# Side transfers on GpSimd's queue, idle products in the outset, and accumulating stores at the end of a one-core S4 and FFN kernel

## The chip, the core and the metric

The kernel runs on one NeuronCore of a Trainium2 chip. Its engines work from their own instruction streams: TensorE (PE in the profile, with the weight loads as PEld), VectorE (DVE), ScalarE (ACT), GpSimd (POOL) and SyncE (SP, which here only issues transfers). A transfer between HBM and the on-chip memory is issued by SP, ACT or POOL, in the order of that engine's stream, and carried out by 16 DMA engines that all queues share. The metric is the device time of one execution in microseconds (us). A second view of the same program, one profiled execution, gives the trace from which all rows here come.

## The reference: what is computed

The input is u of 2048 rows (positions) and D = 576 channels, all float32. With xn the layernorm of u along its channels, the output is the sum of three terms:

```python
x = A_u
xn = _layernorm(x, axis=-1)
return x + _A_ref(xn, A_A_re, A_A_im, A_B_re, A_B_im, A_C_re, A_C_im, A_log_dt, A_Dskip) + _B_ref(xn, B_w1, B_w2)
```

`_A_ref` is a long convolution per channel: a kernel K[d, l], the real part of a sum over 128 complex exponentials, is convolved causally with xn through a Fourier transform of length 4096, and xn times Dskip is added. `_B_ref` is a feed-forward layer, silu(xn w1) w2, with 4608 hidden units.

## The kernel before, in words

**The main stream** is the feed-forward layer, the generator `ffn()`. The hidden units are 36 tiles of 128, taken in 9 chunks of four; the rows are two halves of 1024, each of two blocks of 512. For each chunk and block, `up` makes `ph` = w1 times the transposed xn (L289 to L291), ScalarE takes silu and rounds it (`gf` L297, `gh` L298), VectorE keeps the rest (`gl` L299), and `down` multiplies with w2 into `po` (L318) and adds it to the accumulator `acc` (L323), which began as x itself. float32 operands are split into a high and a low part, with three products for one: that is what `w1h`, `w1l`, `gh`, `gl` are. From the third chunk of the second half on, `wino_ffn` takes the layer with fewer, larger products (lines 427 to 577; weight splits L361 and L362, products L444 and L450, sums `f` such as L519 and L535).

**The side stream** is the generator `side()`, drawn by `weave` at set shares of the main stream's 276 steps. It makes, in this order: layernorm and transposes of x (`phase0`, with `norm`, `normed`, `put_xt`); the convolution kernel (`natural`, `kgen`), whose results go from a `stage` tile to the HBM table `d1k` (L883), while `spread` takes the normalised rows `xr` (L145), transforms them (`u`, L155 to L157) and stores them in `d1u` (L158); 32 spectral steps, which load `ur` and `kr`, multiply, and store `d` (L942); and the tail, which loads `ys` (L993) and makes the last transform, `conv` (L1005).

**Where the halves end.** After the last chunk of the first half `down` stores each accumulator to an HBM table `dr0` (L326), and every second time loads the next pair of x tiles into the freed buffer (L328 through L166). In the tail `load_r0` (L951) brings `dr0` back, `add_conv` adds the convolution to it on VectorE (L1016), and `store` writes the output (L173), 16 tiles of rows in quarters of 32 partitions. The second half's output tiles get their convolution within PSUM: `down` begins `po` with it in the last pass (L305 to L310).

**What sets the order.** The program text gives the order, and the Tile framework's planner (`schedule_with_timeline_sim=True`) moves instructions of each engine within it by its own estimates; `behind(ins)` keeps an instruction after another one, and a pool's number of buffers says how early a load may start. Within an engine, and within a queue, the order is then fixed: an instruction that waits holds up all behind it. SP's queue carries the weights (`w1r` L244 to L246, `w2r` L266), the x tiles, the stores `dxt` (L226) and `dxn` (L227), `xr`, the bases `eb` (L776), `d1k`, `dr0`, `ur`, `kr`, `ys` and part of the output; POOL's queue carries the constants, the very first `w1r`, `d1u`, `d`, the `w` of the second half (L471), the spectral matrices (L892) and output. Dskip is added into one row of `d1k` by an accumulating transfer of POOL (L886).

**The outset.** `side` loads two pairs of x tiles, takes the statistics (L182), scales them (`xn`, on VectorE for even tiles, L191, on ScalarE for odd ones, L196), and PE transposes them (`pt`, L123 and L127), from which ScalarE and VectorE take `xh`, `xl` and the last 64 channels (L124 to L129). Meanwhile `ffn` loads and splits the first weights (`split_w1`, L257 and L259).

```python
    sd = side()
    next(sd)
    fg = ffn()
    next(fg)
    next(sd)
    weave(fg, 276, sd)
```

## Time and profile before

| | |
|---|---|
| time, median of three runs | 1136.37 us (1135.81 to 1136.94) |
| the profiled execution | 1141.59 us, span 1139.8 us |
| granted TensorE clock, mean | 0.990 |
| busy: PE, DVE, ACT, POOL | 1104.0, 955.5, 721.1, 113.4 us |
| moved by the DMA engines | 176.04 MB, mean 154 GB/s |

The span is the time from the first to the last thing that the trace shows; the execution took 1.8 us more. Busy time counts an engine's instructions, not its waits and not the issuing of transfers by SP and ACT; on POOL the issuing shows as busy time, since the engine writes the descriptors itself. A row of the page names line, engine, operation, destination <- sources, and a count; "idle before" is what its engine waited for. The clock column is what the chip's throttle granted to TensorE, as a share of full speed.

### The profile page before, as it was taken

Reading aid. Unit: us, or ns where it says so; the run is one execution under the profiler, and the core shown is the slowest. Engines: PE = TensorE matmul, PEld = TensorE weight load, DVE = VectorE, ACT = ScalarE, POOL = GpSimd, SP = SyncE. Lnnn points to the kernel's source line nnn. Section 1 sums busy time; section 2 is a strip of 40 time slices with the busy share of each in tenths; the row PEclk is TensorE's granted clock in tenths of the full one; section 3 lists DMA queues with packets and bytes.
Section 4 is the critical chain, followed back from the end, with each engine's and each line's share of the span. In section 5 each row is a group of like instructions: output and inputs, shape, how many; then the busy total and the mean of one; then the engine's idle time right before and its main releaser. Section 6 shows DMA issues by size and latency. Waiting matters only on the chain.

```text
span 1139.8 us, 23099 instructions
## 1 busy us (share of the span) xinstructions
PE 1104.0 (97%) x9101; PEld 991.5 (87%) x9101; DVE 955.5 (84%) x1631; ACT 721.1 (63%) x1269; POOL 113.4 (10%) x206
## 2 busy tenths in 40 slices
PE   6999999999999999999989999999999999999798
PEld 5998989888988899899988889999989899998576
DVE  6698898999999999999979988988888888884432
ACT  4665456676677666676747646887867777772210
POOL 1001000000000000000000002112112112210111
PEclk9999999999999999999989999999999999999899
DMA  9456523536263625376844137556455556547964
GB/s 274 131 160 197 165 97 101 144 109 167 83 166 108 188 86 150 109 218 215 230 124 115 54 64 219 153 172 181 141 161 148 171 171 187 176 121 180 260 172 109
DMA packets 171405, 176.04 MB, mean 154 GB/s; under 512 B 88432, under 2 KB 136576, under 8 KB 170656
## 3 DMA queue, kind: packets, MB, share of 16 engines
q1 hardware_dynamic: 150128, 120.91, 38.4%
q0 software_dynamic: 20784, 52.76, 14.7%
q8 instruction: 72, 1.18, 0.4%
q10 hardware_dynamic: 384, 0.89, 0.3%
q14 instruction: 37, 0.30, 0.1%
HBM read 112.00 MB, written 62.60 MB: 153 GB/s over the span
## 4 chain that ended last, share of the span: by engine, by line
PE 52%; DVE 21%; DMA 10%; issue 7%; ACT 7%; SPq 1%; POOL 1%; DVEq 0%; ACTq 0%; POOLq 0%
PE po L318 23%; PE ph L289 12%; DMA w1r<-in_B_w_dram 5%; PE pb L444 3%; DVE acc L323 2%; PE kp L855 2%; PE pc L444 2%; DMA w2r<-in_B_w_dram 1%; DVE th L798 1%; DMA ys<-d 1%; DVE S L834 1%; DVE C L834 1%; PE pb L986 1%; PE pu L986 1%; DVE gl L299 1%
## 5 line engine op out<-in xcount | busy, mean ns | idle before, releaser
L318 PE MATMUL po<-w,gh 128*128 128x288 f32 x2304 | 479.5, 297 | 8.2 <-ACT gh L298 3.8
L318 PEld LDWEIGHTS po<-w,gh 128*128 128x128 f32 x2304 | 378.2, 189 | 26.7 <-issue 5.6
L318 PE MATMUL po<-w,gl 128*128 128x288 f32 x1152 | 337.3, 297 | 0.4 <-DVE gl L299 0.4
L318 PEld LDWEIGHTS po<-w,gl 128*128 128x128 f32 x1152 | 216.2, 189 | 3.9 <-issue 1.4
L323 DVE TENSOR_TENSOR acc<-po,acc 128x288 f32<-128x288 f32 x296 | 130.5, 451 | 61.9 <-PE po L318 60.6
L289 PE MATMUL ph<-xh,w1h 128*128 128x512 f32 (+1 forms) x368 | 99.7, 389 | 0.9 <-ACT xh L124 0.6
L289 PE MATMUL ph<-xl,w1h 128*128 128x512 f32 (+1 forms) x368 | 99.3, 387 | 0.0
L289 PE MATMUL ph<-xh,w1l 128*128 128x512 f32 (+1 forms) x368 | 98.1, 383 | 0.0
L297 ACT ACTIVATE gf<-ph 128x512 f32<-128x512 f32 (+1 forms) x92 | 53.1, 577 | 48.8 <-PE ph L291 36.0
L289 PEld LDWEIGHTS ph<-xl,w1h 128*128 128x128 f32 x368 | 67.7, 192 | 12.9
L289 PEld LDWEIGHTS ph<-xh,w1l 128*128 128x128 f32 x368 | 66.8, 190 | 12.0
L289 PEld LDWEIGHTS ph<-xh,w1h 128*128 128x128 f32 x368 | 65.5, 192 | 11.3 <-ACT xh L124 0.9
L814 ACT ACTIVATE c<-th,magic 128x1040 f32<-128x1040 f32 x36 | 42.0, 1168 | 39.8 <-DVE C L835 31.6
L158 POOL DMA_DIRECT2D d1u<-u x32 | 17.3, 542 | 460.2 <-ACT u L157 460.2
L299 DVE TENSOR_TENSOR gl<-gf,gh 128x512 fp32r<-128x512 f32 (+1 forms) x92 | 60.6, 660 | 2.9 <-ACT gh L298 2.7
L298 ACT CAST gh<-gf 128x512 fp32r<-128x512 f32 (+1 forms) x92 | 55.2, 601 | 10.2 <-PE po L318 9.0
L816 ACT ACTIVATE c<-th 128x1040 f32<-128x1040 f32 x36 | 38.7, 1074 | 31.1 <-DVE th L815 31.1
L361 ACT CAST w1h<-w1r 128x512 fp32r<-128x512 f32 (+2 forms) x56 | 34.5, 619 | 37.1 <-DMA w1r<-in_B_w_dram 36.0
L892 POOL DMA_DIRECT2D m<-in_cm_dram x64 | 34.5, 539 | 223.7 <-PE pu L986 140.3
L362 DVE TENSOR_TENSOR w1l<-w1r,w1h 128x512 fp32r<-128x512 f32 (+2 forms) x56 | 38.3, 685 | 21.7 <-ACT w1h L361 21.7
L834 DVE TENSOR_TENSOR S<-th,C 128x1024 f32<-128x1024 f32 x36 | 43.9, 1219 | 9.8 <-ACT th L817 9.7
L461 DVE TENSOR_TENSOR gl<-gf,gh 128x512 fp32r<-128x512 f32 x56 | 37.8, 687 | 10.8 <-ACT gh L460 10.5
(268 smaller groups left out, 2372.2 us busy)
## 6 DMA issues: line engine op xcount, KB each, us to landing
w1r<-in_B_w_dram SPq DMA_DIRECT2D x35, 512.0 KB, 4.2
dw<-w SPq DMA_DIRECT2D x28, 576.0 KB, 4.7
w<-dw POOLq DMA_DIRECT2D x28, 576.0 KB, 5.8
w2r<-in_B_w_dram SPq DMA_DIRECT2D x44, 288.0 KB, 5.0
d1u<-u POOLq DMA_DIRECT2D x32, 288.0 KB, 2.7
d1k<-stage SPq DMA_DIRECT2D x18, 512.0 KB, 7.0
ur<-d1u SPq DMA_DIRECT2D x32, 288.0 KB, 4.0
kr<-d1k SPq DMA_DIRECT2D x32, 288.0 KB, 3.0
```

Source lines behind the costliest of these rows:

```text
L289: nc.tensor.matmul(ph, w[:, kt, :], v[:, kt, a:e], start=n + kt == 0, stop=False)
L297: nc.scalar.activation(gf, ph, AF.Silu)
L298: pins["gh"] = nc.scalar.copy(gh, gf).ins
L299: pins["gl"] = nc.vector.tensor_sub(gl, gf, gh).ins
L318: pins["pe"] = nc.tensor.matmul(po[:, :HD], gs[g][:, js], ws[:, w, hs], start=n == 0 and j not in begun, stop=n == 3 * len(terms) - 1, ski ...
L323: nc.vector.tensor_add(acc[j][:, hs], po[:, :HD], acc[j][:, hs])
L362: nc.vector.tensor_sub(l[:, :k], src, h[:, :k])
L444: pins["pe"] = nc.tensor.matmul(dst, a[:, kt], v[:, kt], start=start and n == 0, stop=stop and n == 5, skip_group_check=True).ins
L461: pins["gl"] = nc.vector.tensor_sub(gl, gf, gh).ins
L814: nc.scalar.activation(c65, th, AF.Identity, bias=magic)
L816: nc.scalar.activation(c65, th, AF.Abs)
L834: nc.vector.tensor_mul(ov3, t[:, :, 0:64].rearrange("n d (x y) -> n d x y", y=32), mv3)
```

## The change

- Off SP's queue and onto POOL's go the loads of `xr` (16) and `eb` (18), the stores of `dxt` (8), `dxn` (9) and `d1k` (18), and the loads of x at the end of the first half (16). The very first `w1r` goes the other way.
- `dr0` and its loads go. At the end of the first half the accumulators are stored into the output itself, by POOL. The tail's convolutions are made in pairs of tiles, copied from PSUM to a tile `yt` (two buffers) by ScalarE, and stored by POOL with an accumulating transfer, which adds to what the output holds.
- The last pass begins its `po` in other PSUM pools, for two pairs differently.
- Outset: the first pair of x is loaded tile by tile, both of its tiles are scaled on VectorE, and the other x tiles are loaded later; 14 products of a zero matrix run on PE ahead of the first transposes and 5 more after each of the first two tiles; `ffn` and `side` take turns in finer steps, w2 is loaded ahead of the split of w1, and some splits are kept behind other tiles' casts.

```diff
--- before.py
+++ after.py
@@ -81,7 +81,6 @@
     dxn = dram.tile([P, NJ, D], F32, name="dxn")
-    dr0 = dram.tile([8 * P, D], F32, name="dr0")
...
@@ -116,15 +115,16 @@
 
-    def put_xt(xh, xl, x4, src):
+    def put_xt(xh, xl, x4, src, low=None):
...
         nc.scalar.copy(xh, pt)
-        nc.vector.tensor_sub(xl, pt, xh)
+        with behind(low):
+            nc.vector.tensor_sub(xl, pt, xh)
         pt = pss.tile([P, 512], F32, tag="pss", name="pt4")
-        nc.tensor.transpose(pt[:64, :P], src[:, NKT * P:D], ident)
+        pins["pt"] = nc.tensor.transpose(pt[:64, :P], src[:, NKT * P:D], ident).ins
...
@@ -142,7 +142,7 @@
             src = up.tile([P, D], F32, tag="xr", name="xr")
-            nc.sync.dma_start(src, dxn[:, j])
+            nc.gpsimd.dma_start(src, dxn[:, j])
...
@@ -162,15 +162,19 @@
         t = pool.tile([P, 2, D], F32, tag=tag, name=f"{tag}{j}")
-        for ps, v, eng in quarters(xv, engines):
-            eng.dma_start(t[ps], v[:, j:j + 2])
+        for i in range(j, j + 2, 1 if j == 0 else 2):
+            for ps, v, eng in quarters(xv, engines):
+                if j == 0:
+                    eng.dma_start(t[ps, i], v[:, i])
+                else:
+                    eng.dma_start(t[ps], v[:, j:j + 2])
...
 
-    def store(t, j, engines):
+    def store(t, j, engines, **more):
...
         for ps, v, eng in quarters(ov, engines):
-            eng.dma_start(v[:, j:j + 2] if len(t.shape) > 2 else v[:, j], t[ps])
+            eng.dma_start(v[:, j:j + 2] if len(t.shape) > 2 else v[:, j], t[ps], **more)
...
@@ -187,7 +191,7 @@
         for i, j in enumerate(js):
-            if j % 2 == 0:
+            if j % 2 == 0 or n == 1:
...
@@ -200,18 +204,28 @@
         if j0 < 8:
-            xs = load_x(j0, accp, "acc", (nc.sync, nc.scalar) if j0 < 4 else (nc.sync,))
+            xs = load_x(j0, accp, "acc", (nc.sync, nc.scalar) if j0 == 0 else (nc.sync,))
             acc.update(zip(js, xs))
+            yield
...
         if j0:
-            normed(p0, js, xs)
+            with behind(pins["xt1"] if j0 == 2 else None):
+                normed(p0, js, xs)
         else:
-            for j, xj in zip(js, xs):
-                normed(p0, (j,), (xj,))
+            xn = [norm(p0, (j,), (xj,)) for j, xj in zip(js, xs)]
+            last = pins["xn"]
+            for j in js:
+                turned(p0, (j,), xn[j], None if j else last)
+                pins[f"xt{j}s"] = pins["xt_s"]
+                with behind(pins["pt"]):
+                    for _ in range(5):
+                        nc.tensor.matmul(idle[:, :P], zero, zero, start=True, stop=True)
...
     def normed(p0, js, xs):
-        xn = norm(p0, js, xs)
+        turned(p0, js, norm(p0, js, xs))
+
+    def turned(p0, js, xn, low=None):
...
@@ -219,12 +233,12 @@
                 xh, xl, x4 = xts[b]
-                put_xt(xh[:, :, c], xl[:, :, c], x4[:, c], xn[:, i, :])
+                put_xt(xh[:, :, c], xl[:, :, c], x4[:, c], xn[:, i, :], low)
...
                 put_xt(xt[:, 0:4, :], xt[:, 4:8, :], xt[:, 8, :], xn[:, i, :])
-                nc.sync.dma_start(dxt[b - 2][:, :, jj * P:(jj + 1) * P], xt.bitcast(F32))
-        nc.sync.dma_start(dxn[:, js[0]:js[0] + len(js)], xn[:, :len(js)])
+                nc.gpsimd.dma_start(dxt[b - 2][:, :, jj * P:(jj + 1) * P], xt.bitcast(F32))
+        nc.gpsimd.dma_start(dxn[:, js[0]:js[0] + len(js)], xn[:, :len(js)])
...
@@ -240,7 +254,7 @@
             fs = slice(f * P, (f + 2) * P)
-            eng = nc.gpsimd if first and t == 0 else nc.sync
+            eng = nc.sync
...
@@ -253,7 +267,7 @@
                 src = r1[:, :, i * P:(i + 1) * P]
-                with behind(pins.get("gh", pins["xt1s"] if t else None)):
+                with behind(pins.get("gh", pins["xt1s" if t + i else "xt0s"])):
...
@@ -303,8 +317,9 @@
             if half == 1 and c == NCH - 1 and jj % 2 == 0:
-                for i, (pool, tag) in enumerate(((ps2, "ps2"), (ps1, "ps1"))):
-                    begun[j + i] = [pool.tile([P, 512], F32, tag=tag, name="po") for _ in range(2)]
+                pools = (((ps2, "ps2"), (pss, "pss")), ((pss, "pss"),) * 2) if jj == 0 else (((ps2, "ps2"),) * 2, ((ps1, "ps1"),) * 2)
+                for i in range(2):
+                    begun[j + i] = [pool.tile([P, 512], F32, tag=tag, name="po") for pool, tag in pools[i]]
...
@@ -322,10 +337,9 @@
             if half == 0 and c == NCH - 1:
-                rows = slice(j * P, (j + 1) * P)
-                nc.sync.dma_start(dr0[rows, :], acc[j])
                 if j % 2:
-                    acc[7 + j], acc[8 + j] = load_x(7 + j, accp, "acc", (nc.sync,))
+                    store(pairs[j - 1], j - 1, (nc.gpsimd,))
+                    acc[7 + j], acc[8 + j] = load_x(7 + j, accp, "acc", (nc.gpsimd,))
...
@@ -336,10 +350,12 @@
             load_w1(0, 0, t)
+        yield 0
+        for t in range(FT):
+            load_w2(0, 0, t)
...
             split_w1(0, 0, t)
-        for t in range(FT):
-            load_w2(0, 0, t)
+        yield 0
...
@@ -624,7 +640,7 @@
 
-    kl = yp = pa = kfp = tail_at = None
+    kl = yp = pa = kfp = tail_at = zero = idle = None
...
@@ -773,7 +789,7 @@
                     bases.append(kg.tile([P, 2, W, 4], F32, tag="eb", name="eb", bufs=2))
-                    nc.sync.dma_start(bases[-1].rearrange("n g c k -> n g (c k)"),
+                    nc.gpsimd.dma_start(bases[-1].rearrange("n g c k -> n g (c k)"),
...
@@ -880,7 +896,7 @@
                     for gp_ in range(2):
-                        nc.sync.dma_start(kv[gp_, :, :, d0:d0 + NRUN * CH], stage[gp_ * 64:(gp_ + 1) * 64])
+                        nc.gpsimd.dma_start(kv[gp_, :, :, d0:d0 + NRUN * CH], stage[gp_ * 64:(gp_ + 1) * 64])
...
@@ -946,24 +962,19 @@
 
-        r0s = {}
-
-        def load_r0(j):
-            r0s[j] = yp.tile([P, 2, D], F32, tag="r0", name="r0", bufs=2)
-            nc.sync.dma_start(r0s[j], dr0[j * P:(j + 2) * P, :].rearrange("(i p) d -> p i d", p=P))
-
         def last(j):
-            add_conv(j, r0s[j - j % 2][:, j % 2, :])
-            conv_load(j + AHEAD)
-            if j % 2:
-                store(r0s[j - 1], j - 1, (nc.gpsimd,))
-
-        steps, at = [], tail_at[0]
-        for j in range(8):
-            for f in (conv_load, load_r0)[j >= AHEAD:2 - j % 2]:
-                steps.append((at, f, j))
-                at += tail_at[1]
-        steps += [(tail_at[2] + j * tail_at[3], last, j) for j in range(8)]
+            y = yp.tile([P, 2, D], F32, tag="yt", name="yt", bufs=2)
+            py = [[pool.tile([P, 512], F32, tag=tag, name="py") for pool, tag in pools]
+                  for pools in (((ps2, "ps2"), (pss, "pss")), ((pss, "pss"),) * 2)]
+            conv((j, j + 1), py)
+            for i in range(2):
+                for h in range(2):
+                    nc.scalar.copy(y[:, i, h * HD:(h + 1) * HD], py[i][h][:, :HD])
+                conv_load(j + i + AHEAD)
+            store(y, j, (nc.gpsimd,), accum_op=ALU.add)
+
+        steps = [(tail_at[0] + j * tail_at[1], conv_load, j) for j in range(AHEAD)]
+        steps += [(tail_at[2] + j * tail_at[3], last, j) for j in range(0, 8, 2)]
...
@@ -1007,26 +1018,25 @@
 
-    def add_conv(j, dst):
-
-        py = [pss.tile([P, 512], F32, tag="pss", name="py") for _ in range(2)]
-        conv((j,), (py,))
-        for h in range(2):
-            hs = slice(h * HD, (h + 1) * HD)
-            nc.vector.tensor_add(dst[:, hs], py[h][:, :HD], dst[:, hs])
-
...
     def side():
-        nonlocal s4, kl, yp, pa, kfp, tail_at
+        nonlocal s4, kl, yp, pa, kfp, tail_at, zero, idle
         marks = (0.1357, 0.613, 0.855)
-        tail_at = (0.893, 0.003, 0.930, 0.005)
+        tail_at = (0.893, 0.003, 0.932, 0.005)
         with tc.tile_pool(name="pa", bufs=4) as pa:
+            zero = pa.tile([P, P], F32, name="zero", bufs=1)
+            nc.vector.memset(zero, 0.0)
+            idle = ps2.tile([P, 512], F32, tag="ps2", name="idle")
+            for _ in range(14):
+                nc.tensor.matmul(idle[:, :P], zero, zero, start=True, stop=True)
...
                 with behind(pins["xt3"] if js[0] > 2 else None):
-                    phase0(pa, js)
+                    for _ in phase0(pa, js):
+                        if js[0] <= 2:
+                            yield 0
...
@@ -1044,7 +1054,8 @@
                         with behind(pins["gl"]):
-                            phase0(pb, (j, j + 1))
+                            for _ in phase0(pb, (j, j + 1)):
+                                pass
...
@@ -1070,11 +1081,9 @@
 
-    sd = side()
-    next(sd)
-    fg = ffn()
-    next(fg)
-    next(sd)
+    sd, fg = side(), ffn()
+    for g in (sd, fg, sd, fg, sd, fg, sd):
+        next(g)
...
```

## The prediction

> **What bounds the kernel now.** I read the busy shares of the page first, then a table of busy time by stretch, and then, only in the stretches where TensorE (PE) is not full, the chain of work, the waits and the time line of the issuing queue.
>
> ```profile
> PE 1104.0 (97%) x9101; PEld 991.5 (87%) x9101; DVE 955.5 (84%) x1631; ACT 721.1 (63%) x1269; POOL 113.4 (10%) x206
> ```
> ```profile
> 0.00:20.00 20.00, 9.75 (x47) 8.77 (x47) 11.05 (x32) 8.75 (x16) 4.67 (x11) 1.00 0.95 264
> 80.00:100.00 20.00, 18.09 (x102) 15.37 (x101) 16.25 (x35) 9.51 (x17) 1.00 (x1) 0.94 0.65 189
> 560.00:580.00 20.00, 17.00 (x226) 14.96 (x224) 14.94 (x21) 10.92 (x16) 0.55 (x1) 0.97 0.72 221
> 580.00:600.00 20.00, 19.72 (x110) 18.58 (x111) 17.23 (x27) 10.54 (x18) 1.08 (x2) 0.86 0.21 59
> 820.00:840.00 20.00, 17.98 (x103) 16.13 (x102) 14.27 (x29) 13.20 (x29) 3.14 (x6) 0.91 0.38 112
> 1040.00:1060.00 20.00, 18.85 (x150) 15.16 (x148) 6.08 (x13) 2.41 (x5) 1.96 (x4) 1.00 1.11 247
> 1060.00:1080.00 20.00, 12.47 (x81) 9.14 (x82) 9.31 (x21) 5.56 (x11) 3.06 (x6) 0.83 1.04 257
> 100.00:560.00 460.00, 458.59 (x4480) 413.32 (x4479) 437.47 (x660) 305.41 (x458) 19.88 (x35) 1.00 0.50 148
> ```
>
> The columns of the table are busy time (and instructions) of PE, its weight loads, DVE, ACT and POOL, then granted clock, DMA share and GB/s. PE is the bound: in the 460 us between 100 and 560 it idles 1.4 us. What a change of queues can win lies in four places. A stretch loses its idle time and, where the clock is below 1.00, about that part of its busy time: 0 to 20 loses 10.3 us; 80 to 100 1.9 idle + 0.06 x 18.1 = 3.0; 560 to 600 3.3 + 0.5 + 2.8 = 6.6; 1040 to 1080 1.2 + 7.5 + 2.1 = 10.8. A fifth, 820 to 840 (2.0 + 1.6 = 3.6), is touched by no edit. The profiled execution took 1141.59 us with a span of 1139.8, which is 5.2 above the median of the runs; I sum differences against the span and take them off the median.
>
> **The outset.** The time line of the first 20 us:
>
> ```profile
> 1.97 0.81 POOL L244 DMA_DIRECT2D w1r<-in_B_w_dram  x1
> 5.75 1.54 DVE L182 BATCH_NORM_STATS2 st<-acc 128x6 f32<-128x288 f32 x4 [4.82 <-DMA acc<-in_A_u_dram]
> 8.91 1.12 PE L123 MATMUL pt<-ident,xn 128*128 128x128 f32 x4 [8.91 <-DVE xn L191]
> 11.03 1.35 ACT L257 CAST w1h<-w1r 128x640 fp32r<-128x640 f32 x2 [0.22 <-DMA w1r<-in_B_w_dram]
> 12.92 2.07 PE L289 MATMUL ph<-xh,w1h 128*128 128x256 f32 x8 [0.57 <-ACT xh L124]
> 19.08 0.38 ACT L297 ACTIVATE gf<-ph 128x256 f32<-128x256 f32 x1 [2.46 <-PE ph L291]
> 19.31 0.72 PE L289 MATMUL ph<-xh,w1l 128*128 128x256 f32 x4
> ```
>
> Eight such products take 2.07 us at 12.92, and four take 0.72 at 19.31 (eight would be 1.44): until about 19 PE runs at about half speed. The page's clock says 1.00 there, so I go by durations. Two things are late: x (first statistics at 5.75) and the first weights (11.03). Before, two pairs of x (1.18 MB) are asked for ahead of, or beside, the first w1r; after, one pair (0.59 MB), split by tile, so at the 264 GB/s of the stretch 0.59 / 0.264 = 2.2 us less stands ahead. I take the weights and the first products 2.5 us earlier. The idle products cost 14 x 1.12 / 4 = 3.9 us at the slow rate, inside PE's 8.9 us of idleness, and keep PE busy up to the transposes; the 10 others cost 10 x 0.28 = 2.8 slow, some 1.5 fast, in gaps where PE waits for the casts. The work from 12.92 to 18.8 is nearly 6 us at the slow rate; at the fast one, by 1.44 / 2.07, it would be 4.0, less whatever waits then show (the low halves of the weights are split on DVE behind the tiles, and are late next). So 2.5 + 2.0 + 0.5 for a first tile that no longer waits for its partner = 5 us, between 2 (only the data) and 8 (both, with no waits). The memset of the zeros, the extra DMA issues (8 of 72 KB instead of 4 of 144 KB for the first pair) and w2r ahead of the split cost issue time on SP alone.
>
> A row and a rule: the durations change rate near 19 us, 6 us after the products began at 12.92 and with gaps before. The Trainium skill, TensorE: Matmul & The Clock Gate (Part 1), says that the array runs at half rate until it has been busy for about 3.4 us. By it 14 products of 3.9 us just open the gate, and the sum stays; what the rows leave open is whether a gap behind them shuts it again.
>
> **The layernorm of the later tiles (80 to 100).** Chain, then waits:
>
> ```profile
> 79.09 8.09 DMA dxt<-xt
> 91.78 4.15 DMA w2r<-in_B_w_dram
> ```
> ```profile
> ACT xt L124 <- DMA dxt<-xt: 7.4, 2, 6.1
> PE po L318 <- ACT w L275: 1.7, 1, 1.7
> ```
>
> One xt buffer is stored by SP before the next may be written, and w2r stands behind dxt on the queue. After, dxt and dxn go by POOL, so w2r waits for xj loads alone. ACT's wait for the landing stays (one buffer still). I take 2 of the 3.0 us, between +4 (other small waits on dxt too) and a loss of 3 if POOL's store lands later.
>
> **The end of the first half (560 to 600).** Queue of SP, chain, waits:
>
> ```profile
> 563.44 1.00 SPq L326 DMA_DIRECT2D dr<-acc  x1
> 568.85 3.07 SPq L166 DMA_DIRECT2D acc<-in_A_u_dram  x4
> ```
> ```profile
> 573.41 4.97 DMA w2r<-in_B_w_dram
> ```
> ```profile
> ACT w L275 <- DMA w2r<-in_B_w_dram: 6.9, 1, 6.9
> PE po L318 <- ACT gh L298: 3.3, 1, 3.3
> ```
>
> SP stores an accumulator, must wait until that has landed before it loads the next x into the same buffer, and the w2 rows of the next chunk stand behind: SP issues a store at 563.44, the load only at 568.85, w2r at 573.41. ACT waits 6.9 us for it, its gate ops (L298) stand behind in order, PE idles 3.3 and is throttled after. After the change SP has only weights here and runs ahead. The same chain (16 stores of 144 KB, 16 loads) is on POOL, with xr, eb, d1k and d1u behind it: the next late thing would be d1u, for which ACT's next u copy waits (one u1 buffer). I take 4.5 of the 6.6: the rest stays with d1u. Ends: 6 and 0.
>
> **The tail (1040 to 1080).** Chain, waits, SP's queue, the DMA engines in 1030 to 1080, and the landing of today's output stores:
>
> ```profile
> 1040.16 14.89 DMA ys<-d
> 1055.07 10.61 DMA w1r<-in_B_w_dram
> ```
> ```profile
> ACT w1h L361 <- DMA w1r<-in_B_w_dram: 20.9, 1, 20.9
> PE pb L450 <- DVE f L519: 8.1, 1, 8.1
> ```
> ```profile
> 1035.35 0.60 SPq L953 DMA_DIRECT2D r<-dr  x1
> 1039.49 0.62 SPq L953 DMA_DIRECT2D r<-dr  x1
> 1040.16 10.35 SPq L993 DMA_DIRECT2D ys<-d  x6
> ```
> ```profile
> DMA packets 7737, 11.59 MB, mean 232 GB/s; under 512 B 546, under 2 KB 6254, under 8 KB 7734
> ```
> ```profile
> out_dram<-r POOLq DMA_DIRECT2D x16, 144.0 KB, 6.0
> ```
>
> Two r loads stand with the ys ahead of the last w1r; the DMA engines move 232 GB/s at a share of 1.04 to 1.11, so this is bytes. Without the two r (1.18 MB) w1r lands 1.18 / 0.232 = 5.1 us earlier. PE gets there sooner too: the first conv pair comes with tail_at 0.932, and one conv and twelve output products that ran ahead of the wait now stand behind it (order of PE's instructions); that takes back about 2. Half the throttled time (2.1) goes with the shorter wait. 5.1 - 2 + 1.4 = 4.5. Ends: 8 (the bytes of the other r loads help as well) and 0 (the first accumulating store, 0.59 MB that is read and written, stands in the same saturated stretch: 2 x 0.59 / 0.232 = 5.1 us). Copies on ACT (16) take the place of sums on DVE (16 x 0.45); both engines are under half busy there. The 8 stores of dr go (2.4 MB written, with its 2.4 MB read); the stores into the output stay as many, half of them earlier, and 16 come new as accumulating ones. The third copy waits for the first store's landing, since yt has two buffers; the distance between pairs (four steps of 0.005 x about 1130 us are some 11 us) covers a landing of 6.0. If it does not, ACT's gates stand behind it.
>
> **What moves to POOL.** The landing of d1u, then rows of the lines concerned with the issue time in ns (min/median/max):
>
> ```profile
> d1u<-u POOLq DMA_DIRECT2D x32, 288.0 KB, 2.7
> ```
>
> ```profile
> L158 POOL DMA_DIRECT2D d1u<-u x32: 539/539/552, 184.5 to 647.4; - x32
> L886 POOL DMA_DIRECT2D d1k<-in_A_Dskip_dram x1: 858/858/858, 671.8 to 671.8; - x1
> L883 SPq DMA_DIRECT2D d1k<-stage x18: 617/1770/4145, 218.7 to 664.0; - x18
> L244 POOL DMA_DIRECT2D w1r<-in_B_w_dram x1: 808/808/808, 2.0 to 2.0; - x1
> L246 POOL DMA_DIRECT2D w1r<-in_B_w_dram x1: 560/560/560, 3.3 to 3.3; - x1
> ```
>
> L244 on POOL has 512 runs, L246 64: 0.25 us for 448 runs, 0.56 ns a run. d1k<-stage has 4096 runs of 128 B: 0.53 + 4096 x 0.56 ns = 2.8 us each, 18 x 2.8 = 50 us; dxt (1152 runs) 1.2 us, 8 x 1.2 = 9; 16 xr, 18 eb, 9 dxn and 16 acc loads by about 0.55 give 32; the 32 stores to the output replace 16, 16 x 0.5 = 8, and 16 x 0.37 more where they accumulate. All is some 100 us on an engine that is busy 113 of 1140. On PE's path this is worth nothing while d1u leaves in time: the 32 copies of u come from 184.5 to 647.4, one in 14.9 us (in places closer, down to 8), d1u lands in 2.7, and two d1k ahead of it are 5.6, together 8.3, so 0 to 1 us late each of 9 times. Both ends: SP itself takes up to 4.1 us for one, so POOL can be the quicker one, -2; and 9 x 4 = 36 us if descriptors of POOL took 1 ns a run or more. I take 1 us of loss. xr and eb are loaded into one of two buffers ahead of their use, which covers a delay of a step; without it they wait as d1u does.
>
> SP loses 80 of 340 instructions, all between weights; in the full stretches that is worth nothing, since PE idles 1.4 us in 460. The new order of all later instructions, planned anew, has no price in the trace: between +2 (that 1.4 and the like of it) and -6 (one new stall of the size at 560); I take -2. The new PSUM tags of the last pass and the convs in pairs change the order behind 1100 us: 0, between -2 and +1 (a 64-row conv switched in half as often).
>
> **Sum.** 5 + 2 + 4.5 + 4.5 - 1 - 2 = 13 us; I take 12, a part of each first gain being given back by the next wait. Span 1139.8 - 12 = 1127.8; median 1136.4 - 12 = 1124.4.
>
> **Rivals.** (1) Slower: POOL's queue is late. If one d1k takes over 5 us of POOL's time (1.1 ns a run, twice my slope), two of them hold d1u past the next u copy; ACT waits, the gates behind it wait, and PE idles. 9 x 3 = 27 us lost against 13 + 1 gained: 1136.4 + 13 = about 1149. It decides from some 1.6 us a pair on. For it: one u1 buffer and ACT in order; against it: POOL is busy 10% now. (2) The lock: POOL's issues are held up by work of DVE. L158 took 539 to 552 ns in 32 cases beside a DVE that is busy 95% of its time there (437 of 460), so no sign; held by one DVE instruction (437.47 / 660 = 0.66 us) the two d1k and the d1u of each round would leave 2 us later, 9 x 2 = 18, half of it beside other work: 9 of the 12 gone, about 1133. The Trainium skill, SBUF — State Buffer, in the box on "DVE blocks DMA" (section SBUF: two separate sides), says that DMAs from GpSimd cannot get their descriptors written while VectorE runs an op that takes both ports, and advises the other queues: it speaks against the change, and this trace does not bear it out. (3) The tail does not gain: the accumulating stores put back the bytes. 12 - 4.5 = 7.5 gained: about 1129. (4) The outset stays bound by DVE and ACT behind the data: 12 - 4 = 8, about 1128. (5) All gains come near their upper ends, 8 + 4 + 6 + 8 - 1 = 25: about 1112.
>
> **How the numbers follow.** A difference under 0.2% (2.3 us) is no change by the spread of the runs (1135.81 to 1136.94). Forecast, 1118 to 1127: 0.40. (3) and (4), to 1132: 0.25, of which 0.03 no change. (5): 0.10. (2): 0.04, (1) or a new stall of its size elsewhere in the planned order: 0.21, of which 0.04 end within 0.2% and 0.17 beyond. So faster 0.76, same 0.07, slower 0.17. The range leaves out half of (5) and the far half of (1): 1110 to 1141; the forecast's own is 1118 to 1127.
>
> **What would show it.** Outset right: first products near 10 us, the first SiLU near 14 to 15. Weights right: no wait of ACT on w2r near 570, and PE full from 560 to 600. Tail right: the last w1r lands some 5 us earlier and DVE f L535 follows. Wrong: ACT waits for u on d1u with POOL issues of d1k over 5 us; a new idle stretch of PE between 100 and 560; ACT copies of yt that wait for a store.

## The result and the profile after

The changed kernel takes 1141.74 us (median of 11 runs, 1136.29 to 1147.48) beside 1136.34 (1132.36 to 1139.02, 11 runs) of the kernel before. The ratio is 1.0051, with a 95% interval of 1.0031 to 1.0072: slower by about 5 us, where I had forecast 1124.4 in a range of 1110 to 1141. A second comparison (e10 below) gave 1.0037 (1.0020 to 1.0054). The two first profiled executions hide this: 1141.59 us before, 1140.47 after, because the one of before was slower than all its plain runs. A second trace of the kernel before (e0) has a span of 1136.4 us, and I compare with that one too.

Busy shares and DMA packets of the changed kernel:

```profile
PE 1103.6 (97%) x9149; PEld 995.2 (87%) x9149; DVE 950.7 (83%) x1616; ACT 723.7 (64%) x1284; POOL 195.2 (17%) x304
...
DMA packets 85645, 173.68 MB, mean 153 GB/s; under 512 B 10224, under 2 KB 49792, under 8 KB 84896
```

The kernel before had 171405 packets, 88432 of them under 512 B. The table by stretch, with the columns of the one before (PE, PEld, DVE, ACT, POOL, granted clock, DMA share, GB/s):

```profile
0.00:20.00 20.00, 16.83 (x114) 15.84 (x114) 11.71 (x33) 8.64 (x18) 3.95 (x10) 1.00 0.87 251
80.00:100.00 20.00, 20.00 (x116) 17.59 (x116) 17.57 (x34) 12.03 (x19) 2.79 (x4) 1.00 0.60 175
100.00:120.00 20.00, 17.98 (x118) 16.22 (x116) 19.88 (x41) 9.57 (x18) 4.38 (x6) 1.00 0.65 223
280.00:300.00 20.00, 18.17 (x245) 16.82 (x244) 16.84 (x26) 12.74 (x21) 1.82 (x3) 1.00 0.38 112
340.00:380.00 40.00, 36.65 (x461) 32.58 (x461) 36.40 (x56) 26.21 (x39) 3.48 (x6) 1.00 0.34 101
560.00:580.00 20.00, 20.00 (x238) 18.12 (x237) 18.86 (x30) 13.40 (x20) 10.84 (x17) 1.00 0.87 208
580.00:600.00 20.00, 18.27 (x122) 16.39 (x121) 18.09 (x28) 13.60 (x23) 3.24 (x8) 1.00 0.40 124
1040.00:1060.00 20.00, 19.23 (x130) 15.44 (x129) 6.07 (x11) 6.67 (x14) 4.31 (x6) 1.00 1.13 252
1060.00:1080.00 20.00, 13.18 (x98) 11.08 (x98) 5.54 (x12) 4.54 (x11) 1.92 (x4) 0.83 0.46 113
100.00:560.00 460.00, 451.42 (x4436) 405.33 (x4435) 431.80 (x652) 296.92 (x449) 72.92 (x101) 1.00 0.48 147
```

Two of the four places that the prediction named are repaired: 80 to 100 is full at full clock, and 560 to 600 idles 1.7 us at full clock instead of 3.3 at 0.97 and 0.86. The tail's stall between 1060 and 1080 stands much as it was. And the long full stretch, where 1.4 us were idle in 460, now has 8.6 idle, in pieces of 0.4 to 1.8 us that were not there, the largest at 107, 294, 355 and 360 us.

The outset, from the time line:

```profile
7.09 0.66 PE L122 MATMUL pt<-ident,xn 128*128 128x128 f32 x4
11.14 0.72 PE L303 MATMUL ph<-xh,w1h 128*128 128x256 f32 x4
14.05 0.38 ACT L311 ACTIVATE gf<-ph 128x256 f32<-128x256 f32 x1 [0.90 <-PE ph L305]
20.51 0.63 PE L122 MATMUL pt<-ident,xn 128*128 128x128 f32 x4 [1.60 <-DVE mb L198]
26.22 0.56 PE L333 MATMUL po<-w,gh 128*128 128x288 f32 x3
```

The first SiLU is 5.0 us earlier than before (19.08), and the first products run at the full rate (four in 0.72). It earns nothing: tiles 2 and 3, asked for behind the weights, are late (PE waits 1.60 us ahead of the transposes at 20.51), and the first output product comes at 26.22 where it came at 23.6 before. The busy time of PE in the first 20 us contains the 24 products of zeros. Nor does the full rate always last. In the second trace of the changed kernel (e10 below) the granted clock is 0.60 from 20 to 24 us and 0.55 from 24 to 28, behind the same wait of 1.60 us, and eight products at 22.89 take 2.08 us. The prediction had left open whether a gap shuts the gate again; in five of the seven traces that have the idle products, the granted clock of the first 60 us is 0.94 or 0.97. In all kernels without them it shows as 1.00, in a column that doesn't show the slow start.

The tail, chain and waits of PE:

```profile
1040.96 13.21 DMA ys<-d
1054.19 11.01 DMA w1r<-in_B_w_dram
```
```profile
PE po L333 <- DVE acc L338: 6.9, 1, 6.9
```

The last w1r still takes 11.01 us to land behind the ys. Next come GpSimd's side, with ScalarE's wait for d1u (whole span) and the rows of the lines that issue d1u (L158) and d1k (L899), landing last:

```profile
ACT u L157 <- DMA d1u<-u: 13.5, 4, 5.5
```
```profile
L158 POOL DMA_DIRECT2D d1u<-u x32: 545/572/602, 194.4 to 646.0; - x32
...
DMA to landing us min/median/max: 2.4/3.8/15.2
```
```profile
L899 POOL DMA_DIRECT2D d1k<-stage x18: 1626/1648/1691, 213.9 to 668.6; - x18
```

One d1k store takes GpSimd 1.65 us and not the 2.8 that I had extrapolated; the drop in packets says that its runs of 128 B no longer travel one by one. Yet d1u behind it lands up to 15.2 us after its issue, and ScalarE waits for it.

### The profile page after: what moved, and what is told of

Its sections match the earlier page's. It is cut to its first block, busy times and chain, and to the rows that moved or that the text cites. A ratio compares the mean times of both kernels' runs of the same rounds, so it can differ in the third digit from the quotient of the medians.

```text
span 1138.7 us, 23232 instructions
## 1 busy us (share of the span) xinstructions
PE 1103.6 (97%) x9149; PEld 995.2 (87%) x9149; DVE 950.7 (83%) x1616; ACT 723.7 (64%) x1284; POOL 195.2 (17%) x304
## 4 chain that ended last, share of the span: by engine, by line
PE 56%; DVE 15%; DMA 13%; ACT 8%; issue 6%; POOL 1%; SPq 1%; DVEq 0%; ACTq 0%; POOLq 0%
PE po L333 25%; PE ph L303 13%; DMA w1r<-in_B_w_dram 4%; PE pb L460 3%; DMA d1u<-u 3%; PE kp L871 2%; PE pc L460 2%; DVE acc L338 2%; DMA w<-dw 2%; DMA acc<-in_A_u_dram 1%; PE pu L997 1%; PE pk L997 1%; PE pb L997 1%; PE z L886 1%; DMA ys<-d 1%
## 5 line engine op out<-in xcount | busy, mean ns | idle before, releaser
L303 PEld LDWEIGHTS ph<-xl,w1h 128*128 128x128 f32 x368 | 66.9, 188 | 12.6
L831 DVE SCALAR_TENSOR_TENSOR th<-c,th 128x1040 f32<-128x1040 f32 x36 | 44.4, 1233 | 2.3 <-ACT c L830 2.3
L988 ACT CAST yh<-ka 128x576 fp32r<-128x576 f32 x32 | 21.6, 676 | 37.0 <-DVE ka L934 36.9
```

Source lines behind the costliest of these rows:

```text
L303: nc.tensor.matmul(ph, w[:, kt, :], v[:, kt, a:e], start=n + kt == 0, stop=False)
L831: nc.vector.scalar_tensor_tensor(th, c65, MAGIC, th, op0=ALU.subtract, op1=ALU.subtract)
```

## The experiments

The edits are given against the kernel that each text names. All ratios are to the kernel before, run on the same chip beside it, with 95% intervals.

**e0, the kernel before again.** No edit.

> The kernel before, unchanged, for a second trace. Its first profiled execution took 1141.59 us where eleven plain ones have a median of 1136.34, and the changed kernel's profiled one 1140.47 where its median is 1141.74; so the two first traces make the change look 1 us faster, and the runs 5 us slower. If the first trace of before was simply a slow one, this has a span near 1134.5 and less lost in one of the four places (80 to 100, 560 to 600, 820 to 840, 1040 to 1080). If profiling itself costs about 4 us here, the span is again near 1139 with the same losses. Ratio to before 1.000, within 0.002.

Measured: 1136.93 us, ratio 0.9986 (0.9968 to 1.0003), span 1136.4. PE still idles 3.6 us at 574 and 8.8 at 1054, so the places of loss are those of the first trace. The ratio of these two identical kernels is 0.14% off 1, and its interval reaches 0.3%: a ratio of 0.998 by itself is no gain that can be told from this.

**e1 and e2, the d1k stores.**

```diff
 # e1, in the changed kernel (e2 is the reverse, in the kernel before)
-                        nc.gpsimd.dma_start(kv[gp_, :, :, d0:d0 + NRUN * CH], stage[gp_ * 64:(gp_ + 1) * 64])
+                        nc.sync.dma_start(kv[gp_, :, :, d0:d0 + NRUN * CH], stage[gp_ * 64:(gp_ + 1) * 64])
```

> The changed kernel with only the 18 d1k stores put back on SyncE's queue. Theory A (the d1k stores fill GpSimd's queue, d1u lands behind them, 15 us in the worst case, ScalarE's next copy of u waits 13.5 us in all, and TensorE falls idle near 290 and 350): those waits go, landing of d1u is back at 2.7 median and under 7, and the time falls by 4 to 8 us to 1134 to 1138. Rival B (the planner's new order of the middle, not the queue, makes the new stalls): ScalarE's wait goes but other stalls of the same sum stand elsewhere, 1140 to 1143.

> The kernel before with only the 18 d1k stores moved to GpSimd's queue. Theory A: d1u lands late (over 10 us at worst), ScalarE waits for it, and the time rises by 4 to 8 us, to 1140 to 1144. Rival B: the wait is absorbed, and the time is 1136 with a spread of 2 us that the new order makes.

Measured: e1 1140.91 us, ratio 1.0017 (1.0000 to 1.0034); e2 1136.12, ratio 0.9980 (0.9964 to 0.9996). The price of theory A falls by e2: with d1k alone on GpSimd's queue the kernel is not 4 to 8 us slower. Nor is it shown to be faster: e0, the same kernel as before, came out at 0.9986 beside the same runs. e1 lies 2 to 4 us under the changed kernel by the ratios, but its order is another from about 340 us on, so that it decides nothing. The order of e2 differs too, between 336 and 672 us. ScalarE's waits in e2:

```profile
ACT u L157 <- DMA d1u<-u: 16.4, 6, 4.8
ACT w L275 <- DMA w2r<-in_B_w_dram: 11.2, 7, 2.2
```

It does wait 16.4 us for d1u, more than in the changed kernel. But its longest wait for w2r, 7.3 us in e0, is 2.2 here. That is not because w2r leaves earlier: at the half's end it is issued at 573.33, behind the stores of the accumulators and the loads of x as before, and in e0 at 570.84. In e2's order ScalarE has copies of u and gates to do ahead of that cast. So the wait that I feared is real and is paid back, but e2 doesn't tell the freed queue from the other order.

**e3 and e4, the outset alone, in two orders.** Both add the whole new outset to the kernel before. They differ in one line:

```diff
 # e4 against e3
-                with behind(pins.get("gh", pins["xt1s" if t + i else "xt0s"])):
+                with behind(pins.get("gh", pins["xt1s"] if t else None)):
```

> The kernel before with only the new outset (x tile by tile, idle products, first w1r on SyncE, other order of the streams). My prediction had 5 us of gain from it. From the trace of the changed kernel: the first products come 1.8 us and the first SiLU 5 us earlier, but tiles 2 and 3 of x, asked for behind the weights, are late, and at 60 us some 1.2 us are left. By that the time is 1134 to 1136; by the prediction 1131; if only the new order of the middle counts, anything from 1133 to 1139 with the first 60 us still 1 us ahead.

> The kernel with the new outset alone, but with the one line on the splits of the first w1 (kept behind the first tile's cast or the second's) as it was. With that line the planner gives every engine the order of the kernel before from about 140 us on; without it (the run of the outset alone, 1147.2 us) all engines are in another order to the end. Rival B, the order that the planner makes: the time is 1135 to 1137, the outset itself worth 0 to 1 us. Rival C, the outset itself harms (its idle products, the late tiles 2 and 3, or heat that the throttle answers): the time stays at 1144 to 1149.

Measured: e3 1147.23 us, ratio 1.0078 (1.0055 to 1.0101); e4 1138.25, ratio 1.0014 (0.9994 to 1.0034). So the outset by itself is worth nothing or a small loss. The 7 us between e3 and e4 come from one line that keeps back two casts of the first weights, in the first 12 us: with it the planner writes another order for every engine, to the end, where e4 has the order of the kernel before from about 170 us on. In e3 PE idles 3.9 us at 901, far behind any edit, because a w1r that is issued at 895 takes 7.2 us to land and ScalarE's casts for the spectral step stand behind its split.

**e5, half's end and tail alone.** The edits of the diff to `dr0`, `down`, `tail`, `add_conv`, `store` and the PSUM pools of the last pass, with the x loads at the half's end on GpSimd.

> The kernel before with only the end of the first half and the tail changed: no table for the first half's sums, the sums stored into the output, pairs of convolutions added by accumulating stores, x loaded there by GpSimd. The planner keeps the order of all else. My prediction: 4.5 us at the half's end and 4.5 in the tail, so 1128; from the changed kernel's trace the half's end gains 3 to 4, the tail 1 to 3 and the last pass 2 to 3: 1128 to 1132. If the accumulating stores put back what the r loads cost, and the first half's stores delay d1u: 1135 to 1137.

Measured: 1131.68 us, ratio 0.9954 (0.9939 to 0.9969).

**e6, no idle products.** The changed kernel without the zero tile and both loops over `idle`.

> The changed kernel without its 24 idle products and without the zero tile; the order of everything behind the first tiles stays the same on every engine. If the products earn what I gave them (the first work at the full rate), it is 1 to 3 us slower than the changed kernel's 1141.7: 1143 to 1145. If the gap behind them or the late tiles take it back, the time is the same within 1 us. If they only stand in the way, 1140.

Measured: 1140.57 us, ratio 1.0027 (1.0009 to 1.0045), beside 1.0037 and 1.0051 with them. The idle products earn nothing that can be measured.

**e7, the other queue moves.** The kernel before with `nc.gpsimd` for `nc.sync` at `xr`, `eb`, `dxt`, `dxn` and the half's end x loads.

> The kernel before with the loads xr and eb, the stores dxt and dxn, and the loads of x at the half's end moved to GpSimd's queue, d1k left on SyncE's. By my prediction 2 us of gain at 80 to 100 and part of the 4.5 at 560 to 600, 1132 to 1134. By rival B the planner's order, which this edit changes from the layernorm on, decides, and the time lies anywhere from 1132 to 1146 with stalls in the middle that no queue explains.

Measured: 1137.04 us, ratio 1.0009 (0.9989 to 1.0029). No change.

**e8, half's end and tail with d1k on GpSimd.** The edits of e5 and e2 together.

> The kernel before with two parts: the half's end and tail of the change, and d1k on GpSimd's queue. If the parts add up, 0.9954 x 0.998 = 0.9934, near 1129. If the half's end gains the same few us in both (with d1k gone from SyncE's queue the w2 rows come in time too, the run with d1k moved lost 2.1 us at 560 to 640 in place of 5.7), the d1k part adds nothing and the waits for d1u cost: 0.995 to 0.999.

Measured: 1131.38 us, ratio 0.9943 (0.9923 to 0.9964). The product of the two, 0.9934, lies in the interval, and so does 0.9954 alone: what d1k adds here can't be told.

**e9 and e12, all but the outset, in two orders.** e9 is the changed kernel with the old outset. e12 adds to it one line of the new one:

```diff
 # e12 against e9
         if j0:
-            normed(p0, js, xs)
+            with behind(pins["xt1"] if j0 == 2 else None):
+                normed(p0, js, xs)
```

> The changed kernel with the old outset, all else as changed. Sum of the parts as measured alone: 0.9954 (tail) x 0.998 (d1k) x 1.0009 (other queues) = 0.994, 1130. If it comes out there, the outset costs the changed kernel its 11 us, by the order that it makes. If the parts that share GpSimd's queue disturb each other (the first half's stores, x loads and d1k ahead of d1u), it is 1.000 or above, and the outset only adds a little.

> All of the change but the outset (0.9951 beside the kernel before), with one line of the outset added: the statistics of tiles 2 and 3 are kept behind the transposed copy of tile 1. From the first tiles on every engine then has the order of the changed kernel, to the end. If that order is the loss: 1.003 to 1.006, 1139 to 1143. If the outset's own work is the loss: 0.994 to 0.997, 1130 to 1133.

Measured: e9 1132.10 us, ratio 0.9951 (0.9933 to 0.9969); e12 1138.63, ratio 1.0024 (1.0006 to 1.0042). From about 35 us on, the instructions of e12 stand in the order of the changed kernel. One line that costs next to nothing where it stands (PE idles 11.4 us of the first 60 without it and 11.0 with it) turns the gain into a loss, through the order. SyncE's queue at the start of the tail, e9 first:

```profile
1028.87 0.60 SPq L245 DMA_DIRECT2D w1r<-in_B_w_dram  x1
1034.03 8.52 SPq L987 DMA_DIRECT2D ys<-d  x12
1051.09 0.39 SPq L243 DMA_DIRECT2D w1r<-in_B_w_dram  x1
```
```profile
1020.71 0.60 SPq L246 DMA_DIRECT2D w1r<-in_B_w_dram  x1
1036.71 8.79 SPq L988 DMA_DIRECT2D ys<-d  x12
1046.33 2.46 SPq L244 DMA_DIRECT2D w1r<-in_B_w_dram  x1
1049.79 1.79 SPq L245 DMA_DIRECT2D w1r<-in_B_w_dram  x1
```

Around the ys the queue has one order in both: a w1r, twelve ys, the next w1r. What differs is how far the feed-forward layer has come when the spectral steps end and let the ys go. In e9 it has begun 258 of its 296 sums of `po` into `acc`, in e12, in the changed kernel and in the kernel before 262. In e9 the ys have landed when the next w1r is issued, and it lands 23.4 us after the first ys was issued (at 1057.4), before PE needs it. In e12 it is issued among ys still on their way and lands after 27.3 us (at 1064.0), with PE waiting. The stretch 1030 to 1080 in both, e9 first:

```profile
1030.00:1080.00 50.00, 48.67 (x360) 41.37 (x360) 22.30 (x43) 18.31 (x40) 9.11 (x13) 1.00 0.84 200
```
```profile
1030.00:1080.00 50.00, 43.42 (x305) 36.27 (x308) 15.79 (x32) 14.01 (x31) 7.45 (x13) 0.93 0.71 162
```

5.3 us of idleness and 0.07 x 43.4 = 3.0 of clock make 8 us here. The ratios differ by 0.0073 x 1136 = 8.3, the two traces by 5.0 (spans of 1132.2 and 1137.2), since e9 loses some of it elsewhere. The kernel before has this stall too: PE is busy for 41.3 us of the stretch (clock 0.93) and in e0 for 40.6 (0.90). So in the tail e9's order wins what the kernel before loses, and e12's order adds no loss there. What the changed kernel loses against the kernel before stands from 60 to 700 us. That stretch in the changed kernel, in e9, and in e15, which is described below and moves only the half's end:

```profile
60.00:700.00 640.00, 625.55 (x5961) 560.54 (x5960) 594.49 (x907) 411.25 (x621) 109.26 (x151) 1.00 0.47 140
```
```profile
60.00:700.00 640.00, 627.39 (x5967) 564.19 (x5966) 591.23 (x899) 410.12 (x617) 110.09 (x151) 0.99 0.48 140
```
```profile
60.00:700.00 640.00, 636.22 (x6040) 572.60 (x6039) 602.13 (x921) 422.47 (x640) 45.47 (x80) 1.00 0.50 146
```

PE idles 14.4, 12.6 and 3.8 us, and 8.1 in e0. The idleness in the middle is thus no mark of the slow order: the fast e9 has nearly as much of it.

**e10, the changed kernel again, and e11, with dxt back on SyncE's queue.** e11 has `nc.sync` for `nc.gpsimd` at the `dxt` store.

> The changed kernel again, for a second trace and a second ratio on the chip of the runs beside it: 1.003 to 1.007 expected. If the stalls near 290, 350 and 580 belong to its order and queues, they stand in this trace too, with waits of ScalarE for d1u of some 10 us in all; if they were chance, they are elsewhere.

> The changed kernel with only the 8 dxt stores back on SyncE's queue. These are the one queue move that by itself gives every engine another order to the end. Direct price by the traces under 2 us. If the order that this move makes is the loss, the time falls to about 1131 to 1136; if the loss is common to all orders of this kernel (queues that collide), it stays at 1140 to 1143.

Measured: e10 1141.66 us, ratio 1.0037 (1.0020 to 1.0054), span 1139.4; gaps of PE at 108, 296, 360, 680 and 1059, and 13.0 us of ScalarE waiting for d1u: these stalls belong to the kernel. The one near 355 does not come again, and of the 1.7 us at 580 to 600 0.7 are left. e11 1139.12, ratio 1.0018 (0.9998 to 1.0037): another order, and a loss between.

**e13 and e14, other orders with and without the outset.**

```diff
 # e13, in the changed kernel
             nc.vector.memset(zero, 0.0)
+            nc.vector.memset(zero, 0.0)
+            nc.vector.memset(zero, 0.0)
```
```diff
 # e14, in e9
-            xs = load_x(j0, accp, "acc", (nc.sync, nc.scalar) if j0 < 4 else (nc.sync,))
+            xs = load_x(j0, accp, "acc", (nc.sync, nc.scalar) if j0 == 0 else (nc.sync,))
...
-            eng = nc.gpsimd if first and t == 0 else nc.sync
+            eng = nc.sync
```

> The changed kernel with two more fills of the zero tile at the start, 0.17 us each on a VectorE that is idle there. The planner writes another order for the stretch from 25 us to some 690 us, the same one as before behind it. If the order of that stretch holds part of the loss, the ratio differs from 1.004 by more than 0.002, to either side; if the order does not matter, 1.003 to 1.006.

> All of the change but the outset, with two pieces of the outset: the first w1r on SyncE's queue, and x tiles 2 and 3 on that queue alone. The order behind the first tiles is that of the run without the outset. If the order is what counts: 0.994 to 0.997. If the late weights or tiles of the outset are the loss: 1.000 to 1.005.

Measured: e13 1136.84 us, ratio 0.9993 (0.9979 to 1.0008); e14 1130.44, ratio 0.9946 (0.9929 to 0.9964). Two superfluous fills make the changed kernel some 5 us faster, by the order of the stretch from 25 to 690 us, where PE idles 10.1 us from 60 to 700 after 14.4 and 12.2; its tail stalls like that of the kernel before. And pieces of the outset under the order of e9 leave its gain as it was.

**e15, e16 and e17, the half's end and the pairs apart from the accumulating stores.** e15 keeps `dr0` and issues its stores and the x loads there by GpSimd; e16 leaves the half's end as before and makes the tail's convolutions in pairs, with VectorE's sums; e17 is both.

```diff
 # e15
-                nc.sync.dma_start(dr0[rows, :], acc[j])
+                nc.gpsimd.dma_start(dr0[rows, :], acc[j])
...
-                    acc[7 + j], acc[8 + j] = load_x(7 + j, accp, "acc", (nc.sync,))
+                    acc[7 + j], acc[8 + j] = load_x(7 + j, accp, "acc", (nc.gpsimd,))
```
```diff
 # e16, in tail(); the PSUM pools of the last pass as in the change
+            conv((j, j + 1), py)
+            for i in range(2):
+                for h in range(2):
+                    dst = r0s[j][:, i, h * HD:(h + 1) * HD]
+                    nc.vector.tensor_add(dst, py[i][h][:, :HD], dst)
+                conv_load(j + i + AHEAD)
+            store(r0s[j], j, (nc.gpsimd,))
```

> The kernel before with the table of the first half's sums kept, but its 8 stores and the 16 loads of x behind them issued by GpSimd, so that SyncE has w2 and the rest there without their waits. My term for the half's end was 4.5 us: 0.996. If the waits come back elsewhere (d1u behind the stores, or w1r's buffer at 820), 0.998 to 1.000.

> The kernel before with only the convolutions in pairs and the other PSUM pools of the last pass; the table, its loads and VectorE's sums stay. From the traces the runs of convolution products take 2.8 us less, and less issue time: 0.996 to 0.998. By my prediction (0, -2 to +1): 1.000.

> The kernel before with the half's end on GpSimd's queue (table kept) and the convolutions in pairs (VectorE's sums kept). If the two gains add up, 0.990, 1125 to 1127, and then the accumulating stores and the path through the output cost some 5 us beside these two. If they overlap, 0.994 to 0.996, and the stores are worth nothing either way.

Measured: e15 1132.22 us, ratio 0.9957 (0.9940 to 0.9973); e16 1131.12, ratio 0.9943 (0.9918 to 0.9967); e17 1127.53, ratio 0.9923 (0.9897 to 0.9950), the lowest ratio of all kernels here. Its interval overlaps those of e15 and e16; the product of the two, 0.990, lies in it, so the gains may add up in full or in part. The stretch 560 to 600 in e0 and then in e15:

```profile
560.00:600.00 40.00, 36.41 (x405) 32.75 (x407) 32.46 (x50) 22.47 (x35) 1.08 (x2) 0.96 0.42 135
```
```profile
560.00:600.00 40.00, 40.00 (x485) 35.78 (x484) 39.17 (x57) 28.63 (x42) 5.63 (x11) 1.00 0.32 102
```

3.6 us of idleness and 0.04 x 36.4 = 1.5 of clock, gone: 5.1, and the ratio says 4.9. For the pairs, a run of convolution products and what follows it, first in the kernel before and then in e16:

```profile
1105.92 0.69 PE L1005 MATMUL po<-ys,s 64*32 64x288 f32 x8
1106.54 0.53 PE L318 MATMUL po<-w,gh 128*128 128x288 f32 x2
```
```profile
1109.12 1.23 PE L1011 MATMUL po<-ys,s 64*32 64x288 f32 x32
1110.29 0.53 PE L319 MATMUL po<-w,gh 128*128 128x288 f32 x2
```

In the kernel before, the 256 records of convolution products stand in 22 separate runs of 8 or 16, in e16 in 11 runs of 8 to 32. From its start to the next product a run of 8 takes 0.62 us, one of 16 takes 0.65, one of 32 takes 1.16: most of a short run is its beginning and end. That is 2.8 us (13.9 in the kernel before, 11.1 in the changed one, without the stall). The ratio says 6.5, between 4 and 9. Where the rest comes from is not shown; e16 also holds the other PSUM pools of the last pass.

## Why the prediction was wrong

The steps in their order, with what the runs measured (shares of 1136.4 us):

- **Outset, 5 us.** Failed. e4 gives a loss of 1.6 (from 0.7 gained to 3.9 lost). The rates and the earlier SiLU came as I said; the step that failed is the addition of the two to 5 us of path. I had taken the first products as the path, where tiles 2 and 3 and the first output product were next: PE waits 1.6 us for these tiles, and the first output product comes 2.6 us later than before. The range for this term ended at 2 and 8 and did not reach 0. The idle products have no measurable worth (e6); the first 14 take 5.8 us (1.15 to 6.99) and not 3.9, as each makes two records.
- **80 to 100, 2 us.** The stall went, as said, but 2.0 us of idleness appeared in 100 to 120, where PE waits for VectorE. All queue moves but d1k give 1.0009 (e7).
- **Half's end, 4.5 us.** Right: 4.9 (e15), by the mechanism named.
- **Tail, 4.5 us by fewer bytes.** Failed. The bytes are gone, but each piece of the sum is smaller. For 5.1 us, 3.5 come: the last w1r lands 28.2 us after the first ys is issued (1037.0 to 1065.2), where it took 31.7 before (1034.0 to 1065.7). For the 2 taken back, 2.4: PE begins to wait 23.0 us after the first ys and not 25.4. For the 1.4 of throttled time, nothing: the clock of 1060 to 1080 is 0.83 before and after. (Half of 2.1 is 1.05, not 1.4.) So 1.1 us are left of the 4.5: PE's wait is 6.9 and 7.8 us (two traces) after 8.1 and 8.8, and the ratios don't show so little. The three parts together give 0.9954, two of them without the accumulating stores 0.9923: the stores and the saved table gain nothing. Whether they cost some 3 us is not settled; the intervals meet between 0.9939 and 0.9950. (Four steps of 0.005 x 1130 us are 23 us and not 11, which only adds to the room for the stores.)
- **Pairs of convolutions, 0 us (-2 to +1).** The term that was most mis-sized in itself: a gain of 6.5 (e16). The 22 short runs stood in the trace of before, and I had not priced a run by its own beginning and end; that is 2.8 us of it.
- **What moves to POOL, a loss of 1.** No gain or loss of d1k alone can be told: e2 gives 0.9980 where e0, the unchanged kernel beside the same runs, gives 0.9986. My slope of 0.56 ns a run was twice the measured one: a store takes 1.65 us and not 2.8, and (1.65 - 0.53) / 4096 is 0.27 ns a run. (SyncE issues 417 transfers before and 327 after; the prediction's 80 of 340 is miscounted, and no term hangs on it.) The wait of ScalarE for d1u came, 10.0 to 16.9 us in all in each kernel with d1k on GpSimd's queue; its worth in time stays open.
- **The new order, a loss of 2 (+2 to -6).** This is the step that decided the sign. The parts alone multiply to a gain: 0.9954 x 0.998 x 1.0009 x 1.0014 = 0.996, about 1131.5. The whole is at 1.0037 to 1.0051, 9 to 10 us above. One line that only changes the planned order makes 8.3 us of difference between e9 and e12, and e13 shows 5 us with the outset in place. I had priced the order by "one new stall of the size at 560", where it is several small ones: PE idles 14.4 and 12.2 us between 60 and 700 where 8.1 were idle before (e0) and 3.8 with the half's end alone (e15). So the gain at the half's end is lost again there, in the fast e9 too (12.6), and the tail keeps its stall, which the order of e9 and e14 avoids.

What the middle's idleness comes from stays open. It is there in every order of the kernel with all the queue moves (10.1 us in e13, 12.3 in e14), and in e1, whose ScalarE has no wait for d1u, PE idles 4.8 us between 140 and 560 where 1.1 were idle in e0. Parts that disturb each other on GpSimd's queue are a rival to the order here, and no run separates the two.

Of the rivals, the first had a clause, "a new stall of its size elsewhere in the planned order", and that is near to what came, in small pieces; its main mechanism (POOL's queue late) came as a wait, without the 27 us that it was priced at. Rival 3 and rival 4, no gain in the tail and none from the outset, were both true at once, which I had priced one at a time. The lock of rival 2 is not to be seen: the 32 issues of d1u took 545 to 602 ns.

Not settled: how the 10 to 11 us between all-but-outset and the whole split between the order and the outset's own loss. e12 leaves 0.0013 to 0.0027 for the second, about as much as e4 measured, and within the intervals of both.

## What to carry to other kernels

Where a planner writes the order, an edit's price has two parts, its own and that of the order it provokes, and the second can be larger: run the edit under two orders (a harmless line is enough to get the second one) before believing either sign. Take a change of several parts apart before keeping it: here two useful parts, the half's end and the pairs, were kept from sight by the rest, and e17, these two alone, gains 0.8%. Compare the whole of two traces before calling a stall the cause: the one in the tail was there before, and the ones in the middle are in fast kernels too. Short runs of small products are priced by the run, not by the product: time a run from its start to the next other product.

## What the runs showed of the hardware

- The short runs travel in fewer packets when GpSimd issues them: with d1k alone moved (e2), 171405 packets become 99981, and 88432 of under 512 B become 14704, with 176.04 MB moved in both. The landing of a d1k store was all the same 7.0 us (median) from SyncE's queue and 9.2 from GpSimd's in the changed kernel (8.5 in e2), and GpSimd's own time was 1.65 us for 4096 runs of 128 B.
- An accumulating store of 144 KB took GpSimd 0.76 to 1.67 us (1.22 median) where a plain one takes 0.49.
- With the same order and the same work behind it, a kernel's stalls move: e6 and the changed kernel have one order from the first tiles on, and PE idles 4.1 us in 560 to 600 in the one (clock 0.91) and 1.7 in the other (1.00).
- Idle products at the start brought the full rate early, and it did not always stay: the granted clock fell to 0.55 in e10 (24 to 28 us) and to 0.50 in e4 (14 to 16 us), with PE busy all the while.
